# Value products of 32x64 tiles issued in six parts per pair, with a new order of issue and a new bank table

## The chip, the cores and the metric

The kernel runs on one core of one Trainium2 chip. The metric is the device time of one execution in microseconds; three runs of the kernel before gave 941.70, 940.48 and 942.59, a median of 941.7. The profile comes from a further execution, of 943.45 us.

## The reference, cut to what matters

Eight batches of eight heads, 576 rows, head size 64, all in float32. Attention keeps only the scores within `tau` of the row's maximum; a gated MLP with a spatial mix follows on the heads put side by side.

```python
scores = q @ k.T / 8
thresh = scores.max(-1) - tau
p = exp(where(scores >= thresh, scores, -1e9) - scores.max(-1))
x = p / (p.sum(-1) + 1e-9) @ v                 # (8, 8, 576, 64), then heads side by side: (8, 576, 512)
h = gelu_tanh(x @ w_in)                        # 1024 wide: u, v = halves
v_n = (v - mean(v)) / sqrt(var(v) + 1e-6) * g_ln
out = x + (u * (w_sg @ v_n + b_sg)) @ w_out
```

## The kernel before, in words

Two heads make a pair, so there are 32 pairs (`n` = 0 to 31), four for each batch. The function `attention(n, g0)` makes the steps of a pair, `moe(b, m0)` those of a batch's MLP. A step is a small closure with a kind: `at(kind, time, fn)` appends it to a list named `plan`. Nothing is issued at that point. At the end `issue(plan)` walks through `ORDER`, a packed table of step numbers written into the file, and calls the closures in that order; each engine's queue gets its instructions in this order and works them off in it. `FIRST_BANKS` is a second packed table that names, for each tile of PSUM in the order of its first use, which of the eight banks it lies in (`bank` one bank, `two_banks` two neighbours). So the order on every engine, the DMA queue of SyncE (SP) among them, is written out by hand ahead of time, and semaphores keep it safe where a tile or a bank is used again.

The pairs 4 to 30, 27 of them, work by rows (`by_rows`). A pair has nine tiles of scores (`scores`, L543: matmuls of 128x128 weights with 288 columns, four or eight for a tile, into two banks). For each tile VectorE (DVE) takes the maximum (L552), GpSimd (POOL) the threshold (L558), ScalarE (ACT) the exponential (L579), DVE the selection with the row's sum (L586), and DVE transposes 32x32 blocks into the tile `turned` (L596), of which there is one buffer. When all nine are there, `turned_values` (L743 to L751) multiplies with `v`: 18 blocks of 32 keys (`NB`), four row groups of 32 partitions (`NG`) and two heads, 144 products with weights of 32x64 and 144 columns, each of which the trace shows as two matmuls and two weight loads. Eight such tiles fill the array side by side. Their sums go to four banks, `accs`, as two tiles of two banks. After the last, DVE scales the sums by the inverse row sums (`scale_turned`, L757), and ACT and POOL split the result into a high and a low part for the MLP. The loads of the next pair's `v` go into the same buffer as this pair's.

The MLP's products (`products`, L843) are issued in steps of up to four matmuls of 128x128 weights with 288 or 512 columns, of kinds v, u, y and o; the order puts them among the steps of attention, so that TensorE (PE) works on the MLP of one batch while the pairs of the next are in the softmax. In the order before, the whole of `turned_values` is one step, and its 288 matmuls follow each other in PE's queue.

Of the kernel before, what the change touches and what calls it, by code (L numbers as in the profile page):

```python
# [32 lines left out]
ORDER = (  # L33
    "c-mE12S8L;7X9ZB^Zo$C0D>Y_!LDG#j%>_oG#V^vx{8_@Q`MN=O-$dIvMH`5MNKqoOpGOoCYp#QF|J0VV#P+W0HPE{Q2H?Q|KPlR<<CF{_~pG@&OP_O`"
    "`(}^3Z+zD_zx5>yRwgbm3LD_ksmoDN5mYvdi@h^MX3}Jzh1OHD~kWwf2Tfa3g0+{IY<~n&8xsG<iK4*g65XxBWNqu){B=rmx9ci*R;omz3fd`;x4_?q="
    "X{nsWixhz1*yn5TP<7Vw7tu)Ms5dU}H=IR5%l4LWsyeel_vPz=cshB;6?j6wGk_iI5@+pAmu*sE=VUq#3U16;`NX`k-bee1IW6Dn7RFz|4plvv45&K|="
    "E(P<${!16^D>P*GgerYKH<T=51ugPcNx+Ss_urcjr^NSGW|niYj<DmLn}xfEM7e>Tww372$Z6L^HW%_ZOqV@!ix`JBtNrAXms8^^&M2z_SRtS@PYicxQ"
    "n%f!HExO=I~KkS(+QI1Jq73iF*FG1X>B2}o6aJ81BO>wHysxye0r2?f)3pGKAfT_RYT{fw2vU*1qR!wv~U}?Z6fbrMXi1?!vpo*=vI9&b(X%iZPUJ;D+"
    "$0exL6?vh)^~W7a$PBJaCW+@vIP|T4Ati|w<~bMswqP^K5bW_ko2zx<3$7Gb+eV;hE*~{*djxlA5-Tyeq!SU0%#nzgN_&Dqtu>R>gr~TCtWZ<kChJHz6"
    "r%Farnp5;IUqkk*}Axd=90!-z6R(^zsZI`EWNp;hM5YP7*W-xd09G&xfV<VRQc1d-?U=pT%nrVEM6*@kr=7J^V+DtZ@Q?z4ivL0SZsnFUn(>=AJyE{AE"  # L40
    "!CaS>QiR*v+Q7nwx5zPPdrUs9T2Rmd&0`xuqFKl#M;|5vI%LxTw4_QB9b2o6h+wo7A|LTanQGo=t1a6qOhy7JqGM;>qn>hYXc8>Gt#CGpD&ZJgXtY(4<"
    "GV=IemmvYY2tar>F%D&kEzWY4B^@hBqo$E^quKC6lhl6$2Bo-`t+-O|7CD6I%<G7ExqO~xa0shQZ!tJ^F_O~lW%1iu0umF%0?ByHS?o61a@D?&0P(&v`"
    "wWoAT9WtsS#2t6v3MEz6<I?P>Nh)4`FZrVz_nKBs&mE~gwtthf|s3bx{lO&kPxqxJo-KpDOl2S`Z`&g5|{xUZK3edh)pvebmUu)$+Fs3QGS@|+4V%qF)"
    "LP(OL6aJt}s}h6a_CfLmpt%)a48Eo&QtUr<h<Y>GqP`j;X5d6Ivnr_4+ti9gMCJPPC6O~DCx~uFF9w((kwV-H(P?V|%VdgQv52KPvwZz)-Xxx9R<ff}-"
    "Ph`fPTXzIZCqV9Q_enw@>k;aZ4Vrnm}4l+JP2K#j}W)7%9$89%&!W+F*Aa0ZpvqcjZq=O-l^_CArfIryb2uL0N0aArGJ7US)qFCNs{Qk!vLpAlhd3(-M"
    "9DfaS;_aEMaj~b6#51iRsK2iP=TP14ko<{BM#Z{@kWFOGXsktQ;aGbRujM37fr8!I6L=p%X!rqWibwHivM|q;zD)C3zsSm<11JZa8utpDwCJ=0YY!#7J"
    "e30=(|uzD3kT#v;chZ^D?2>CY#55tT?EC9Nx@RiFA0`oYT!HzZe|coDEf+&VQm5cxKXPgV|9`~@Wo#(Yp@fhiKZF7|W@O8^urU6w`bb}C<mKS{Q*AWcy"
    "p7NP0OT$}GfK5avIAd0`VsX#?_vsC4vAe9)>2vZWd@HrOoQ=feqoh*Dmod)%7N{WvdQE~oywweotnuTB{l=_+v)qM*?=7}0I(~?i|V=iKyaA#J<paK*1"
    ")quYSiCibtmrUw&q)^3VR1j#@rKBuBvtCSmikxAFt%gL+12DK(_N2>K$_5N`>tSN-#;#Uh3e3gQdWd5&2_t5LtvVCucZ0KIaE6#cVMMr-lycYxZS#H0b"
    "U{sj{KxEi{E;hC;l#?FNmhl5Ap#MTRz;G>B)A#hZYBMiFGlP4Y@chtBN?M%l`jU@5y0E9;yVU$6at}Qz8S(fALKe#6Q_?9L8m$7Ywl)LB4oi8HGB{h>D"  # L50
    "M&p-yRGzMTTs3T+J#oYx?IV1S^JQL5TPbv?*D`w{cK&o<Cbf4RD6|jVD!RQ1D~wOAWJTT6r{NF8<sw|J17d-KnhrZF8r8lJ@U_wDmtCZT^KpX&W!5gzw"
    ")Et^Y&up{A`%z;DnGp8gq2t0CI<zX7eW98)pOOVyK;oX+DzW@ZoVu3kI%wZ#Ht>}esMV8G=Vx-Vo{lk+m^6nqF)fTSNER#YEWKWJ}K6?B`mWzjpY{?Zu"
    "i$W6Kw+O6qkeQI6gh$HGLBmu$YcBlPXV!I-1OJaqB`@f3_Lv~E?lw}=AP)T4&bzsNlgrZL81^}m@zSMlHqIUx#g3hb)<O<xd#VQS<4MwEZYK4ci97RIs"
    "^;6QGUvW6mnOHD(Z8r+_YCmW3T}_37YE)chi8rEKz{R3L(HHyIME=j)wF*Hk<hBj&xSF6l?ts8Mp2)NDg->mbvy<BiKrNxSZ`bwFiw7I8FRitc;NQoTS"
    "<2LC%Yb6<jnv<JdxK*0Y63!&H_is?8}~m_-*~4qHMoBJW6k+Pntm7sVE?28si*I$?SQJnyIWY_+cA;scw=|kab?edPz<`b{lNhrjm4IC4<a=hH*!M5y*"
    "oySdo9hk`hUK#_;$a*3ViknP;g>Ihw2Nx4?S=_wz|XiN2@_fuVv(SB)UfnP#t;Dg3y9ys0Zh+M<gbGnPJ17m>b5f$iI<V;E9ago5{_vZ)dlB^GNNJ6RS"
    "?V6O~_;Tkyr>-vidq=9NbgPXnxuNZ{#3%v9YU7!!MI{oFg&c1<HIF83%&dd&UF4MIF56xFe-o;CjY;nIHt&T<DncyrmS@4tU1;FU+!@Z>)tSd>9=b2i+"
    "M4%OIJZf|#y<-Z#cWt0G~JG<81-lfi7vT)@~UlsOvB>!|lpQh42<*08reh(dwUst|^hO*EG+yO#^D&ra(;wlE?V!b-FJOtj+HMth3r-wFO7}^w2AKnW)"
    "9cX|f?t-JSSH(L&ms?^cthvzlDmvp_bftsk0zEGGal_RYD$~o=Kugi7i&2&vnqJy9kCczWW%OV(hw4LYI?Mio6QqR%e!gte?2T7Z+YX3mng21nbtH!&K"
    "BJ*t>J7J%Z%fSs3kzv^N$Tk#%9&|o?7UtJS9Z(ldJ-egB?lnB#Ci%&jB0eC<ISpYqRyU%gp?zWMrI|_<(j;+CN>#+9_6_78;8`9nd-sM9S`LV+^Kt^2E"  # L60
    "%DbQ^?}C5pPKBIs>-7M~uC2*tV(1dN=K}>67<NJv!q*<Jjc32p~<}F|}}l^@9ghw`vm_YaiXPIBVs|$M@a!VKhRTm<-PL7#5}8j`T*>MqfEF_wKQ;x;`"
    "zL_v_z&c^vZx0u7;GK30$CSc28JU;bkK%!S5V?;BrZBr?@a`2Jzcc%&%wd9paPL0`dS+@FDX=97<}A^FqJ5>G@Evmf;Cv({ceP1(6B=KfvJWBF@wkK>J"
    "i=3sOz){NkH?%>T@9!$ycpEs7cSG=}(V+o>1K~)c)O(t`pLtE5SAg9KVEy&Ec@)a4luaXXfdUO_kgd>Daw&Z8eQ|Y5aPU3TC_?%S{ShjQD7;SHSx#giB"
    "T(fF`aNv&;>q=Ia`+?2GJ|pcpI_EmW=4i}Yuv#5;sJQEu_+e+dI&$u2gQbpSYYSfOT-tT?=Tp)D)oJ}(${Ip}y@OAwmj35}^#2Wpa*FiBQ)^UEduAFCL"
    "qhVC%cfAzuZS&M{m0Ri^JzFXe0A!X)VkmRHRl=ZAAN#|IC`E?lTc~&KRSX506B(pQ26--wKP5eY1u(}-flf{{&HVdf@#<_a5zq&E3QPKD$3DVty0y&n7"
    "N}K#4Il|rX#vCA$<#aCSGNzndv}YjAfyrIaBDnDI>vJ9t{1K!yN}y%W{cAZn!ht84}{Pczaz&vH^01@zC6bO&50?et@(mfZpvON&khJsyvL@4D-PKcGa"
    "TN+K4=E|8LZ?kA#R&%8_t#$gNPrehpai@{%Q2G5ObVMY-X19ugaogZ@Tg%Rnx7azIQOsW-w&3rhcTt+RUqi(x}!P(bl0%YHP+p<l5P*ie?7NDZ~1Y~rR"
    "h8!PJK%QYi|JHg&pa*pb@0X8E$1Z74q#4LZ1!|2--l9!T~a`w9qcx@D&>OOlXGIrJsa25hXPNrJaV`&0oAz$z4l~81lx*TlSiy57>{=UlluONG9bY-+^"
    "xzc3~x&Vv!ll`Oj<I=s^pKWUDPJSPKa!A_I%`DpT>xj8g%p6WFtV5VhN6v^a5@Kko#cB5(8v1S0Uz5kaW8WW^6m0Cmw5<c#y6%mJA0x6BCU2O1R;80F*"
    "cv#CZNNjrJKo$eRx{26Ls@ES3cgQ&`WCXU-$LZG4C=Mcue`l@DGI;OdMXWTmX8Ov=KX8Wy*po9u0Jqh(Xt;fY6XwmF{j;%=dmJT3y|r}m^WqTbhe+~E_"  # L70
    "{JaEiGOP%onMFvAF>R+Wlm!ZpVxqq#B=vvaN8@`nm2kfzK>i`Q}qlqbiN19Z=(#XFM@5Y|f2#wp9V>g+qUt3U%J<SHfStb~yc!r@ZO-BUAO{**D;A^+k"
    "=Kk+qE_g4(_($?MofzX^xBa@SeoWz3BxrG5VSp_{z$QAz=;J&)aJ30{EZD;S6CXa?JCR()#NaOf@z8p0OFJ(^sm2JG9$=x504c9c0o@VevUvW2S`Eej9"
    "KZ2plaHlrpGflIpErnC6Ieq_^-&f8{g=Ho3Sv&a?n-`N}A(i*OX>-t9CjzjEt_)CV&!=<;)z}EY})9!x}D^4RNCu1JdinhX9`^JC0mM6YoM(*2H-@O_x"
    "HSQLkV12bIWW>w3`_q?py@hR4=XAoz|Ne70?#$WvMo)wt5bd+MPk2bf$uVqmIZQ6i-k5oMz}e2%?m{2ndkuP2eOPG95d}H<F*ne)_!+j-V51$FvXl9;u"
    "njb9^J{y@?ob0VejB&jY7rDVJ)y>53%egNYD*@M`z^~m91owupqxR6ZggqiX=`0-bMQr@Tl4rUr9tg0;!5wjikrL!npq>TSTW#4)ZxSFtZT6Tg9=Mw_d"
    "8B|Ocm`2bkc46g4KTR%R}mI=Yvk9<atu8eRktssBA;aQ|JFin*q&moEie;9Zb7K6O#)xi!(Lsgp)Oxb~h5#>rt_dIA`s1!blfwQUf`r#xl$uVosG~NR?"
    "XBH}PuX_YarUbwHOtNdJ=F0bir3FNU62zU^|Y%us%ey(odzA~fXov*1js1)bgHKtN(qi=pPGI$vA$>?c-Pu3BT4yl|&AjyHVhl}P$&%9WtT3sfB%Sz&9"
    "i8%em{*z;0I=7Az~uMbmeZ-z#)5D=_3RnOc!V|N6za=TiqPtNbpJy#WlBAPX+yrF2w*5>X;jmG*nx+JoL!cDdbBa&31Lk?!b*t2qRR1@*YhE~ne)#zw!"
    "XSjkrO;Mg0+$y*SWt}YS%-WKbVQdS#A3xvsbLXDTWmoUL1YTw8##1xBMlM?vgLjV)*yjqm`=l`8NX?JoU6R#h*W&hLP9|5Y_h!tmqx~=R!I_)?upkf35"
    "jfsgh5I6gT3lz79qQ(&^!Va+Lxuz#Juwt1c2)m{Z8rVR_hO8dM+YP{*mpmg6`z2PywR&mBc>zmz}n|mELgq3V_zRv5m)h;d)4NJH7}@i8Nwg`0{GCvI!"  # L80
    "WgHuP@{^^Rb6~8D1Anh-N>Y%wr8u8_D#IL90_kS1;J#ooz5x50To#lQ|FTLz?Dp2(;C`P*xuvpw{+%^DXzSJx{!iH{UlN`F7Wl3%!lyi<V8p+7Dit`W$"
    "nyot=?T6Y<>A$@}q@$`+j5u2u5<-fv>sy$eiEV7>ai*BOm1FTLZ6gvUd^2ClFbU2=4U%EWb>S{14u938a;b5z~-(bX@1?ykKD-k6J6nm1tVv%{ZX5kBe"
    "3k%vxZwu|Eg=z$M@H7ar2)c4{a`r#p5&-T2?f~?)NaM@gJdT}XRAk*`cf!r;bTUa4X{2+NEel(t{3n%MR{<3N^I^mP6Sa@~tCg{&%z0>xjv6eh-TiW7S"
    ";0Au3{GZ?_v=3QLJcjkglfPxr&uqJ}?w-!;?jkR-lUu{?(wEl-m%>GQqOgYx=LU>AGAKJOXBzOG`ysF|Jl~AW?iYvJcx;)pE0;BjgbKAAnqYS_GVpKpV"
    "{`xHZLpD$iAyGX$WN2TEl41>Q4`tMoo}Z{vmMFdp40g9jH%a8^>CajWYV3PZmuOEeOn8OR|n%H8!AdvM|?eI|7f7Zn9NQ9t~C$rc%UKWU3og}o;&zlG^"
    "_h|*1e=7!uSz0;3hU7S-Wv2-6HxWhUGFU@Ga&#OPcrzf+SwN!Hz&XKiz{P!Gxr0#@>k3)7)4U85N>46V}FK@i#k;-!S~3EjChbs_3T=K43viw#x_`e2X"
    ";3UAMbq?ChHt+@2)?!;jE4=a7=!qtSYB7G2*nx{{q!yu2mkGyk1NvcvMBTOFuc7INRu81CGX!luro#PEJl`Hy)PIub<_D}S0)UlYihO@V7riF?HHMu*y"
# [20 lines left out]
WARM = 4  # L110
# [1046 lines left out]
```

## Time and profile before

| | |
|---|---|
| median of three runs | 941.7 us |
| profiled execution | 943.45 us, its span 941.5 us |
| PE busy | 849.7 us (90%) |
| DVE busy | 701.0 us (74%) |
| ACT busy | 605.4 us (64%) |
| POOL busy | 587.1 us (62%) |
| mean granted PE clock | 0.978 |
| value products, PE | 7,776 matmuls, 146.9 us busy, 56.4 us idle ahead of them |

The span runs from the first to the last instruction. Busy time is the union of an engine's instructions; matmuls overlap each other, and their ends are modelled, so a matmul listed with 0.28 us can be followed by the next after 0.016 us. "Idle before, releaser" is the time in which an engine did nothing ahead of an instruction and what ended it; "issue" means that nothing the profile shows ended it.

### The profile page before, as it was taken

The page shows a single profiled execution, that of the slowest core. Times are in us where ns is not written, and L with a number is a line of the kernel's source. Part 1 is how long each engine was busy: PE and PEld are TensorE (multiplying, and loading weights), DVE is VectorE, ACT ScalarE, POOL GpSimd, SP SyncE. Part 2 cuts the span into 40 slices and gives each one's busy share as a digit, 9 for nine tenths or more (in the row PEclk, how much of TensorE's full clock was granted, in tenths as well). Part 3 has the DMA queues.
Part 4 walks back from the last instruction along what each step waited for, and adds up shares of the span by engine and source line. Part 5 has one row for each costly group of instructions (what it writes and reads, how often), then busy time and mean ns, then how long its engine had stood idle before and what let it go on. Part 6 is the DMA issues. An engine that isn't in the chain of part 4 may idle for free.

```text
span 941.5 us, 30436 instructions
## 1 busy us (share of the span) xinstructions
PE 849.7 (90%) x12440; PEld 761.2 (81%) x12440; DVE 701.0 (74%) x1436; ACT 605.4 (64%) x989; POOL 587.1 (62%) x973
## 2 busy tenths in 40 slices
...
GB/s 248 177 73 104 130 104 88 149 159 112 156 126 158 169 170 84 117 163 129 145 103 137 125 133 134 162 110 135 127 128 150 139 121 153 99 84 28 32 7 52
DMA packets 71998, 115.79 MB, mean 123 GB/s; under 512 B 10033, under 2 KB 32049, under 8 KB 71858
## 3 DMA queue, kind: packets, MB, share of 16 engines
...
q8 instruction: 98, 1.61, 0.7%
...
## 4 chain that ended last, share of the span: by engine, by line
PE 66%; DVE 10%; issue 10%; POOL 6%; ACT 6%; DMA 1%; SPq 0%; POOLq 0%; DVEq 0%; ACTq 0%
PE all_banks L843 34%; PE all_banks L750 15%; PE all_banks L543 11%; DVE nm L552 3%; DVE p L586 2%; DVE turned L596 2%; PE all_banks L239 2%; PE all_banks L738 2%; ACT p L579 2%; POOL klz L445 1%; PE all_banks L521 1%; POOL ot L1050 1%; ACT L832 1%; DVE ir L757 1%; ACT L579 1%
## 5 line engine op out<-in xcount | busy, mean ns | idle before, releaser
L579 ACT ACTIVATE p<-all_banks,nm 128x576 f32<-128x576 f32 x256 | 184.1, 741 | 91.0 <-DVE nm L552 89.5
L586 DVE SCALAR_TENSOR_TENSOR p<-all_banks,nm,p 128x576 f32<-128x576 f32 x256 | 201.9, 806 | 49.7 <-ACT p L579 29.7
L552 DVE TENSOR_REDUCE nm<-all_banks 128x1 f32<-128x576 f32 x288 | 207.6, 743 | 18.8 <-PE all_banks L543 11.8
L750 PE MATMUL all_banks<-turned,v 32*64 32x144 f32 x7776 | 146.9, 290 | 56.4 <-issue 54.2
L750 PEld LDWEIGHTS all_banks<-turned,v 32*64 32x64 f32 x7776 | 128.4, 133 | 71.9 <-issue 66.9
L596 DVE STREAM_TRANSPOSE turned<-p 128x576 f32<-128x576 f32 x216 | 159.9, 759 | 31.8 <-PE all_banks L750 31.7
L543 PE MATMUL all_banks<-ks,qst 128*128 128x288 f32 x560 | 164.0, 312 | 13.5 <-DVE p L586 9.1
L558 POOL TENSOR_TENSOR nm<-columns,nm 128x1 f32<-128x1 f32 x288 | 53.3, 192 | 188.4 <-DVE nm L552 155.6
L543 PE MATMUL all_banks<-klz,qst 128*128 128x288 f32 x560 | 157.5, 300 | 0.3
L543 PEld LDWEIGHTS all_banks<-ks,qst 128*128 128x128 f32 x560 | 107.8, 192 | 25.5 <-DVE p L586 12.7
L843 PE MATMUL all_banks<-wsh,z 128*128 128x288 f32 (+2 forms) x512 | 112.8, 301 | 1.5 <-DVE p L586 0.7
L543 PEld LDWEIGHTS all_banks<-klz,qst 128*128 128x128 f32 x560 | 108.1, 193 | 2.1 <-POOL klz L445 0.9
L843 PEld LDWEIGHTS all_banks<-wsh,z 128*128 128x128 f32 x512 | 86.6, 193 | 2.8 <-DVE p L586 1.0
L445 POOL TENSOR_TENSOR klz<-rk,khi 64x576 fp32r<-64x576 f32 (+1 forms) x56 | 80.0, 1429 | 8.4 <-PE all_banks L543 2.5
L832 ACT ACT_TABLE_LOAD x52 | 66.7, 1283 | 26.8 <-PE all_banks L843 17.6
L843 PE MATMUL all_banks<-gh,woh 128*128 128x288 f32 (+2 forms) x256 | 76.6, 302 | 0.7 <-DVE p L586 0.4
L843 PE MATMUL all_banks<-gh,wol 128*128 128x288 f32 (+2 forms) x256 | 76.4, 301 | 0.0
L843 PE MATMUL all_banks<-xh,wih 128*128 128x288 f32 (+2 forms) x256 | 75.7, 301 | 0.6 <-ACT vv L832 0.6
L843 PE MATMUL all_banks<-wsl,z 128*128 128x288 f32 (+2 forms) x256 | 75.8, 300 | 0.0
L843 PE MATMUL all_banks<-xh,wil 128*128 128x288 f32 (+2 forms) x256 | 74.9, 297 | 0.0
L843 PE MATMUL all_banks<-xl,wih 128*128 128x288 f32 (+2 forms) x256 | 74.6, 296 | 0.0
L843 PE MATMUL all_banks<-gl,woh 128*128 128x288 f32 (+1 forms) x240 | 71.6, 301 | 0.0
...
## 6 DMA issues: line engine op xcount, KB each, us to landing
...
ks<-khi SPq DMA_DIRECT2D x110, 144.0 KB
...
```

The costliest lines, as they stand in the source:

```text
L239: nc.tensor.transpose(out, x, ident_r.bitcast(F32))
L445: nc.gpsimd.tensor_tensor(klz[h][rows, 0:w], st["k"][rows, o:o + w], st["kh"][rows, o:o + w], ALU.subtract)
L543: nc.tensor.matmul(sc[:, a, 0:HALF], w, x, start=(j == 0), stop=(j == len(terms) - 1))
L552: nc.vector.tensor_reduce(nmax, st["s", h, i][:, :, 0:HALF], AX.XY, ALU.max, negate=True)
L558: nc.gpsimd.tensor_tensor(thr, toff, st["nm", h, i], ALU.subtract)
L579: nc.scalar.activation(target(h, i), st["s", h, i][:, :, 0:HALF], AF.Exp, bias=st["nm", h, i])
L586: nc.vector.scalar_tensor_tensor(dst, st["s", h, i][:, :, 0:HALF], st["thr", h, i], dst, ALU.is_ge, ALU.mult, accum_out=st["l"][:, c:c + 1])
L596: nc.vector.transpose(st["turned"][:, :, o:o + Q], st["p", i][:, c0:c0 + S].rearrange("p (k x) -> p k x", x=Q))
L738: nc.tensor.matmul(acc[h * D:(h + 1) * D, 0:w], st["v"][:, o:o + D], unit(h, a)[:, kt, 0:w] if kt < NM else tail_unit(a)[:, 0:w], start=(k ...
L750: nc.tensor.matmul(accs[g // 2][hs, g % 2, 0:W], st["v"][rows, o:o + D], st["turned"][rows, k, h * W:(h + 1) * W], start=(k == 0), stop=(k ...
L832: put("gelu", end, lambda: nc.scalar.activation(tile_of(), acc_of(), AF.Gelu_apprx_tanh))
L843: nc.tensor.matmul(st["acc"], *term(j), start=(j == 0), stop=(j == n - 1))
```

## The change

`turned_values` takes a range of the 18 blocks of keys, and six steps of three blocks (24 products each) take the place of the one step. The accumulators are taken at the first part and stay until the scaling. The plan grows from 4,543 to 4,678 steps, and both tables are new.

```diff
+PART = 3
...
-        def turned_values():
-            accs = [two_banks(f"pv{n}_{a}") for a in range(2)]
-            for k in range(NB):
-                for g in range(NG):
-                    for h in range(2):
-                        rows, hs = slice(g * Q, (g + 1) * Q), slice(h * D, (h + 1) * D)
-                        o = k * P + h * D
-                        nc.tensor.matmul(accs[g // 2][hs, g % 2, 0:W], st["v"][rows, o:o + D],
-                                         st["turned"][rows, k, h * W:(h + 1) * W], start=(k == 0), stop=(k == NB - 1))
-            st["accs"] = accs
+        def turned_values(k0, k1):
+            def f():
+                if k0 == 0:
+                    st["accs"] = [two_banks(f"pv{n}_{a}") for a in range(2)]
+                for k in range(k0, k1):
+                    for g in range(NG):
+                        for h in range(2):
...
+                            nc.tensor.matmul(st["accs"][g // 2][hs, g % 2, 0:W], st["v"][rows, o:o + D],
+                                             st["turned"][rows, k, h * W:(h + 1) * W], start=(k == 0), stop=(k == NB - 1))
+            return f
...
             if by_rows:
-                at("pv", g, turned_values)
+                for k in range(0, NB, PART):
+                    at("pv", g, turned_values(k, k + PART))
```

What the new order table says of these steps, decoded: in 100 of the 135 seams between two parts of a pair nothing else is on PE's queue. In 35 there are other matmuls: 4 of them in three seams, 8 in seven, 12 in sixteen, 16 in four, 20 in two, and 10, 14 and 18 in one each, 406 in all. Twenty pairs have one such seam, six have two and one has three. In 33 of the seams there are scores of the next pair among them, in the others only products of the MLP. For pair 15, for instance, PE's queue reads: scores (0,0) and (1,0) of pair 16, parts 0 to 2, scores (0,1) and (1,1) of pair 16 (eight matmuls), parts 3 to 5, scores (0,2) of pair 16. The scores (0,1) lie in the banks of the scores (0,0), the scores (1,1) in those of (1,0). In the order before, all four stand ahead of the value products. On each engine the other steps stand on average two to four places from where they stood.

## Rows read from the trace of the kernel before

**Rows 1.** The page's first part: busy us (share of the span) xinstructions.

```profile
PE 849.7 (90%) x12440; PEld 761.2 (81%) x12440; DVE 701.0 (74%) x1436; ACT 605.4 (64%) x989; POOL 587.1 (62%) x973
```

**Rows 2.** The chain that ended last, shares of the span by engine.

```profile
PE 66%; DVE 10%; issue 10%; POOL 6%; ACT 6%; DMA 1%; SPq 0%; POOLq 0%; DVEq 0%; ACTq 0%
```

**Rows 3.** Waits: engine, line, waited for: us in total, times, longest us.

```profile
PE all_banks L750 <- issue: 54.2, 36, 3.0
DVE ir L757 <- PE all_banks L750: 45.6, 17, 4.9
...
DVE turned L596 <- PE all_banks L750: 31.7, 11, 5.5
...
PE all_banks L543 <- DVE p L586: 9.1, 8, 3.0
```

**Rows 4.** Timeline of PE, 643.6 to 655.2: start us, us, what [idle before].

```profile
644.13 2.72 PE L750 MATMUL all_banks<-turned,v 32*64 32x144 f32 x157
648.58 2.25 PE L750 MATMUL all_banks<-turned,v 32*64 32x144 f32 x128 [1.73 <-issue]
653.15 0.46 PE L750 MATMUL all_banks<-turned,v 32*64 32x144 f32 x3 [2.31 <-issue]
```

**Rows 5.** Timeline of PE, 371 to 375.5.

```profile
371.59 2.25 PE L750 MATMUL all_banks<-turned,v 32*64 32x144 f32 x128 [1.12 <-issue]
375.04 0.50 PE L750 MATMUL all_banks<-turned,v 32*64 32x144 f32 x15 [1.20 <-issue]
```

**Rows 6.** DMA queue, kind: transfers, MB, share of 16 engines.

```profile
q8 instruction: 98, 1.61, 0.7%
```

**Rows 7.** Timeline of PE, 184.2 to 192.2.

```profile
184.57 0.29 PE L543 MATMUL all_banks<-ks,qst 128*128 128x288 f32 x1
184.70 0.29 PE L543 MATMUL all_banks<-klz,qst 128*128 128x288 f32 x1
184.93 2.97 PE L750 MATMUL all_banks<-turned,v 32*64 32x144 f32 x173
188.98 2.17 PE L750 MATMUL all_banks<-turned,v 32*64 32x144 f32 x115 [1.09 <-issue]
191.08 0.40 PE L543 MATMUL all_banks<-ks,qst 128*128 128x288 f32 x1
191.32 0.29 PE L543 MATMUL all_banks<-klz,qst 128*128 128x288 f32 x1
```

**Rows 8.** Line L750: duration ns min/median/max, first and last start us, form.

```profile
L750 PE MATMUL all_banks<-turned,v x7776: 277/281/497, 128.6 to 859.3; 32*64 32x144 f32 x200
```

**Rows 9.** By stretch: length; busy (xcount) of PE, PEld, DVE, ACT, POOL; granted clock; DMA.

```profile
163.30:166.70 3.40, 3.40 (x73) 3.02 (x58) 1.23 (x2) 0.00 (x0) 0.00 (x0) 0.51 0.14 14
...
654.90:658.30 3.40, 3.40 (x16) 3.40 (x15) 2.56 (x6) 1.97 (x5) 1.90 (x4) 0.50 0.46 162
658.30:661.70 3.40, 3.40 (x28) 3.40 (x27) 2.85 (x6) 1.93 (x5) 2.28 (x4) 1.00 0.46 116
...
794.80:798.20 3.40, 3.40 (x16) 3.40 (x16) 3.25 (x6) 0.68 (x3) 0.77 (x2) 0.50 0.62 162
```

**Rows 10.** Groups: xcount | busy us, mean ns of one | idle before, releaser.

```profile
L579 ACT ACTIVATE p<-all_banks,nm 128x576 f32<-128x576 f32 x256 | 184.1, 741 | 91.0 <-DVE nm L552 89.5
L586 DVE SCALAR_TENSOR_TENSOR p<-all_banks,nm,p 128x576 f32<-128x576 f32 x256 | 201.9, 806 | 49.7 <-ACT p L579 29.7
L552 DVE TENSOR_REDUCE nm<-all_banks 128x1 f32<-128x576 f32 x288 | 207.6, 743 | 18.8 <-PE all_banks L543 11.8
```

**Rows 11.** By stretch: all 27 value blocks, and a stretch dense on DVE.

```profile
128.60:859.60 731.00, 656.74 (x11180) 610.37 (x11180) 568.11 (x1142) 461.52 (x698) 448.53 (x729) 0.97 0.47 131
300.00:400.00 100.00, 93.58 (x1589) 87.56 (x1588) 84.69 (x171) 72.07 (x109) 69.72 (x113) 1.00 0.51 141
```

More of the change, by code (lines that the diff above doesn't have):

```diff
@@ L33 @@
 ORDER = (
[L34 to L87, printed above, removed]
@@ L88 @@
-    "=jLi9^99DK3szCbT^wSM@XAMGO@XXDz*Lq_5dx417VQu<rR+lRK&@G5VIUYVrn#$0N<)FBu9r?3<Y&VkiY<4)+>Y}uBv6@!LRt973%s@|&TPaN{Vc+ja"
-    "Lj<0hH-+w|NmTWO8Afn?aSMWt7S^F`EO&kLlh@son5)HA?z_jsl!3TwXz60b-~)Ce4WIWR{D|4e*4(iXH)3wYUdUwiyLR(z@9yZz7zd7pT?V@KqQ^!Y1"
-    "^bf9b|+FW6qg*a7yH0%A@#uyutQjSPDG=lPeG5%39K_8pYoHMk<~YAer447wdL{Uh`SgP9L~<&H4%I6jp0eR7IrU;`DA-G8*`G=!*W;@NY2-7m)WMZ9B"
-    ";DfohVL`E5YhGbn&<uz>Lx)3-m?vKXs&KC(%x<G((!VKe&EY7BJEIJI0;>#$iu7U9|fHe*EJ*gx+cC%ob<(&EKM`x`XdYc2*i>+SX}mz!xA|^@P}U>f_"
-    "}n^$|(u$?xdE)Ow)@(bX&aF!~Tf6xjXBod6dh_o>?%M-wJLLlZg{z&=4eKj0S_O>E&RC6ltOxHro^7426qz*jL!W%R72U>*C*n2sQ7*f~0|B`?06ss_N"
@@ L93 @@
-    "xc#LcBX8hObJsWmB7|NO(0(Gi>I%jw0CLp6d@P4pX`^*oxyJPhq$oTB<S9;%cC6+cJ2CmSnTNmR!*t9txM{0&v+*N#~n-sWpQs7UHYPM$B;h7ECAT~1A"
-    "=^osR$O?7<Wv6QEVOGaa0za^_j^zTSKs>**19_(g_7#!IIlBes_GLFVdWp4$Sm!}Zz=hry#^4wn6&S<%+mSIhuAP}v2lLaZ0ZEQ(hrzbO;$B6p3trILJ"
-    "9PW`I8AFT?_!j92`cJ_0`xBNFyT0x&a13R8>bmy^a2+(X{CT&dIA@^mg~K63+_O7AY42ML%RhevL_ZRGyi{avoF&"
+    "c-mE133wCL7M?R{?o65{Z7HQKZCSctX$uGxq#*bN!6%zg5J8`Spnxdiz96`M`rMw%Q)J%+!39*1@(=_!6j@3UC`)%*3bX}E(lp6T(%g6My)$V|!(`^(v"
+    ";5~j=bn29Num;dDF0zs3KFG~`NuBpu74X3-$00&knl>y5M{q046}PS7uE`YsrUj7@qv&zVPY}VxnaCPFA(B$AutfK5iSD)9-lC$@e1L%3{hb`1i}&iGT"
@@ new lines @@
+    "$Iva6uZ9jmUss1$?H3!XawNQV?TcXmgv)1ow%q*ex3|P=kmi1ZLFy4h0NDA?}Ua4YlzjBB2J2T+1*<IR+jo`xgQu8g>zXl9^N^yZphB45!mDz$_aeMWB"
+    "Kh&R)1O@M4oBk0b;+n~V^<m*TM3<^gukP}#gT2?yEL=54Dg{8Ld7A8`u*jPy$E4*$>qDhM}h%428ac<cRp*)e%EYm<EFmm5bp=8(;BV>WJ<-FSr(vuiV"
+    "mK)W70_1gFy$8G1J1PU%|V;ChK6psNPywt2jHbcFf4nEN;GbJyM;l-yi$J`zN^6)s-UTzw(N;V%g3tJK&)1R0B3zxpl2tkBx6FLH^p~>)akE+*ZvSc$8"
+    "=2NMU6De$>h|k7(5jjzjKQ74K(6)3)B1@>@Q@w%)b3q!5m#Tgy!}vEQZ9Z-YBcm9ejVXrLIU~i#t@_L*ErrWlTvT6p+#p5>Q)7x%0k^^9WfSO+&9LYxp"
+    "TRo}m_;qI0UCBgO@q`&)pqVtNj1V@irhN0jdxs(jdD9Glk|llsw{oNITgbykItw1Om~7DHiBa+L*x?xDKqU8Vd0b##>wY|EB;HlPeGDu@FzHtc+kwE>J"
@@ new lines @@
+    "#CZM$~Yp^NF?1af!?^93nL4mkQJEdH{2%a!Us1)bMF0gn=;K8*VsR)C9+5I2tptYM2e-Rghss;uFlZD>+L23gsjyeoEVygR%A%@g$g({HmWN)fa}tlj#"
+    "$2OB}zT+s73-*NVY0k42Cqs@<nZq6FG9$(I%T_|3XE;}rSl!Lk?>zv5?>@QPvz7xfzj!mzL!VnS@f&&9+O=Z-%jNUqC%@mVo==LQ*gKR3%2{Jeuwzi1u"
+    "d8fRKK!iG66W|S%-mqyWZlxU4fay#solc4&AEoQ{e)es)K;GPwZ*=MFf@f&1wLw?$BXAmPidF<Y#LqOr-Q$8w!r((ivfy@m~P&VgRgffC)eDLfmf;>?j"
+    "f*7-Om^;RwB6#u(W)weFOoYOtKiqBwT56tCc!rsG7Nx?=kY(M7htb4SCK;3o=Zg51xNkE(JSGmtOp4#M!f+ZWggTXs#0u7!IWwom0^&k`?p~CGVmgp`h"
+    "9r|3$%sC@QiO9}_guy-Kk-bBYzgy5it(OkOoN(9HIgApkO}a-aCw#(Gs}u(CWbRD7OJ^s+HD&Wvu|=>e!_VXG#KT_tCLW%NJQQ_7h;uANiwU5)1$R*g~"
@@ new lines @@
+    "Z=hpA4tQbI%G`(#+a13PdP~ylG-pn*6sv<%)5%Y(h~qVn7zrVo*4#30oS`SVBd`;HVKS>iETSCY(Qwn<il<xIS$wF2cjpm}wIL<%3*~n5{tZ6S1xd!=x"
+    "Fd&5hv*`@>s;s+x!k!4Z5Q61ObzUn(NgB&jV|2ABLt<5?p#EX37#12VS`{1VE>m^gEa84>=&Cr2XaZ{O4@AEsPR#3u=yhMF0uCSakEh=fm5!y;#h+u@d"
+    "2*lbpq6dW6O91b<gkZ5M#B4(Ltw9OnB5g>W^f=I!aFew-j+(;&JL)%!qglkiie<Q`zh>zK#ta1dyZT#{?5*~q3R#fEH;EtG14I;Q3!jr)5Qf`FuB#Ue?"
+    "dnU7H=uCjS*NBl-Gar)RHM}c}QjsJPH!(1xj8&)9xaYA-Ces|JRnl3TAx1;vj4@MID*O@385c$=uNc9nz}N0*EWA+7EIk7dmlv8wwNtJATd62VUY1&0N"
+    "uipKS1Z5OtsEFb#WO@Doke9XxA2PM(NGlDg&<F~m8HmBio7mF*RZ0H7FMP#T~s%+s<k^m6Vau^z01mMh6~6lYzhtZZq==neF?*%3*L1$h4)sGaz=(2;u"
@@ new lines @@
+    "ot<+g|w?PTiyv1<b<XqiB%|RpC}Q_eB;8^DG>47#Iq3z(80TgOtH)lM(E(8_F>=NhZkrP_D^E*)P*(bhW*hN~SyRglCQl-o@GwKG_X5V&PsSo=I+u=xj"
+    "vz)D4Uhm(h7_lJKav{YOW5k1{|oo~(NKP1CBkdxKym7)qXr@PA_HX0zg?a0;kkQW9}<mu(x4^!H<})b1rE+<na>IW;eBdnj$M@V7T8+O~21&3IV7U7(b"
+    "jhoAQEpl!<LsjQvxzu&cq{0*5U1b@g7il7#NyiP4seg^rL%|||b@y^20KL+gJw+-_YM|d1TH*{zQRa1u?9#rni0(-fO^eI#2%Y%03kzjNMSTd{9j(LV0"
+    ")0LY}4Q^_QYKcBYzzLowziTP5{1B9zQ|lU{2Ub-;y0b!#=}_Zn(eB$8Ogr8&wT^Z<KD>zpsS7$@bCN)f><1zzyQ8gE@VaXH$^McqT}Z<>Pj^NjxffbVl"
+    "ag2Fxsci8j5m_B*5<h~PbVDfeKDhncsjWvgWYP?dR<K+FWfazm814~h#VOJ@WiFm1)~-Hw{b2~9iO?Udjiy7j!tVjkuFE&{?@5%9DFw8tn-?7&YBU`^F"
@@ new lines @@
+    "lXRe@9v04o#k*x4wtFctU_Qcu&ZS*U0hyG;+1ektBeWZ&FSd{0wkMQzsw+@|`DZGHgqh8hVobX(^;*lw;@JJK=caOGVKC&52+Ir|kN1jIE-3^R;nTu5T"
+    "NYVynB*{Ro`_P}=EgY4Bf%NbtynKYC=ibO>6lQji29<QL{P6n=C%rOpcWRt>+u%w7kx))&a&>$VlH73eY64G)6ti|MOp-iRfEEz{-CcMhDjbMlFg@0|k"
+    "Z@vfbS>nd2&pc0hG8-wbXjQ{?PItAno_4YtnPWMt>v3@x<8e*<CEl*hR@)8m`ch!y9mN%cP|Li4a>s$5DgIA8tJ=nb>E_U|EA&}PqTm<`)7dHSDz&G<?"
+    "J>1ih`EltR0E^$G8`%A1d&3WpEqe?;anD~qA3l9?>_30#Esx(Zo)#={cs@P@&PO1LyfFXm7e76G6l4p?H{uF5mkjhp>JOI`O@OaR)0K%Zycrx&*5eaRb"
+    "uV(kW=ogaOejgOeQa5elHMTauL;awn>HLGewwUmpn&$eyYFyV-P#N8Tb!GJ#BUp^0{CE`Mh2{&w{i|GcqRjOz%xzI2<+3?<G0BThkJAY`1y7KT{$!uU@"
@@ new lines @@
+    "5@+-y9lzD2dd(6uoic7b+qf1F&z@u6tqKR8;y#mm{BlPd|1m!#q6jfu&$Oozx2_ww>>l0##$boUZS={pay1XXApfVutd4w_(3QUJ-`((ZW8#sFq;N$0V"
+    "m>LPV7BE0_}VOGz(gCUA!1xyjn=r0fJa1#09BSUXc*50F@&>VN?dI&K;LKRJ7c?8+gT0BHafhwWtaevcj}xa&P;m!{}SYwNB_U-uzFB5P`j0#JEVDJ07"
+    "DN@sfjivUh!*v@ndX{se2;JR`u&nr{;mVN55HS<<JyawI0cpRPt?`g!+C8}AD>i?&r6g?OsJI9@<BMuwDc?)gI4Mm_sO>RkomWr5!Y{X8yXxmCHEjXpf"
+    "`vzHYq~+wWh5uE$SBKK8(*7dZm5KH;Ij0EJ3?Ro9=rLjii@2K{k^g7Dj6DYi9K!|yyT|;>#uJGHz?nXA$42luZ1N;})B=AF##PXgimNO+iN)+b4L3VHK"
+    "aH9H;f|+jQ>sIezSanWy8gZ6=Pum`BNvWycpSsvVm^)`;3F^IKNRNB88g;``zd{s8%Lu6i>nzh>&=zve>u|q=cj+`aZF@<zJL@*O(b7=5Qlr!v+jS9Qv"
```

42 lines of the change are left out of this document (38 added, 4 removed).

## The prediction

> **What bounds the kernel now.** I read the busy line, the chain, the list of waits, then the timeline of TensorE (PE) inside one block of value products, and last the clock by stretch. PE is busy 849.7 of 941.5 us, the next engine, DVE, 701.0 [rows 1]. The chain is 66% PE, and 10% of it is "issue", time in which the engine waited for nothing that the profile shows [rows 2]. So PE sets the time, and its idle time is the thing to look for. The list of waits has one large entry for PE: 54.2 us in 36 waits of L750 on "issue"; the next, scores waiting for DVE, is 9.1 us in 8 [rows 3]. L750 is the line of the value products.
>
> The timeline shows where that is [rows 4]. A pair's 288 matmuls (144 products, each two records) start at 644.13 and run 157 long; PE then idles 1.73 us, does exactly 128, idles 2.31 us, and does 3. Between the idle times lie 128 matmuls with their 128 weight loads: 256 instructions. Another pair shows the same 128 [rows 5]. The instruction queue has 98 transfers of together 1.61 MB, 16 KB each; PE has 24,880 matmuls and weight loads [rows 1, 6], or 254 per transfer. I read the idle times as PE running out of fetched instructions: it consumes a block of 256 in 2.0 us (128 matmuls, 15.6 ns apart: 172 steps in 2.97 - 0.28 us, the length of the last one [rows 7, 8]) and gets a new one only 3.45 us (371.59 to 375.04 [rows 5]) to 4.57 us (648.58 to 653.15 [rows 4]) after the last one began; I use 3.9. In the 128x288 matmuls, 0.13 us apart, a block lasts 17 us, and nothing is missing. The Trainium skill, "Runtime: NRT & Kernel Launch", section "Instruction fetch mechanics", has the same block (16 KiB, 256 instructions), but calls the crossing "mostly hidden"; by that these idle times would have another cause and stay, which is the last rival below. The trace agrees on the block and not on the hiding.
>
> Some stretches right behind such idle times run at half the clock: from 654.90 us PE does 16 matmuls at 0.50, in the next stretch of the same length 28 at 1.00 [rows 9]. I found eight such stretches behind blocks of value products (the first and the last stand in the rows too).
>
> **The change part by part.** The sum is made against the profiled execution (span 941.5 us, 943.45 us in all, 1.75 above the median of 941.7); I carry the difference over to the median.
>
> *The split itself* adds no instruction: six parts of 24 products are the same 144. What counts is where other work enters. Decoded, the new order interrupts the 27 blocks 35 times, with 406 matmuls in all, 12 in the commonest case (16 times), 8 in seven, 4 in three, 10 to 20 in nine; the other 100 seams between parts have nothing in them.
>
> *Stalls removed.* The 36 idle times are counted from the modelled end of the last matmul, 0.28 us after its start [rows 8], while the next should have started 0.016 us after it: 54.2 + 36 x 0.265 = 64 us. With m wide matmuls inside a block, PE takes (128 - m) x 0.0156 + m x 0.132 + 0.40 (the price of the interruption, below): 3.8 us for m = 12, 3.3 for 8, 2.9 for 4. Against 3.9 that leaves 0.1, 0.6 and 1.0 us in place of 1.9. Over the 35 interruptions this is about 9 us. But the block boundary must lie so that the interruption falls between two of them. Counting two instructions per matmul through the new order, with wait instructions as dense as before, nearly every block that lies inside value products holds one; one has none, and several hold only the smaller of two: 14 us remain. If the boundaries fell anywhere, it would be 28. I take 14, from the count: -50 us, bounds -36 and -55.
>
> *The clock.* A half-clock stretch loses 12 matmuls of 0.13 us [rows 9], 1.6 us; eight are 13 us. They follow idle times that mostly go; I take -10, bounds -4 and -13.
>
> *Interruptions added.* On the way in, the first value product starts 0.23 us after the last wide matmul (184.70 to 184.93) in place of 0.13. On the way out the next wide one starts 0.21 us after the last value product (191.15 - 0.28 to 191.08) in place of 0.016, and the one behind it 0.24 us later in place of 0.13 [rows 7, 8]. Together 0.10 + 0.19 + 0.11 = 0.40 us, and 35 of them +14 us, all of it on PE. It is what speaks most against the change: with other work in all 135 seams it would be 54 us and eat the gain. The Trainium skill, "TensorEngine Tiling (Array Packing)", section "Key Properties", says that a change of tiling mode drains the array; the 0.40 us agree, and the page has no price.
>
> *New waits.* In 33 of the 35 interruptions the work put in has scores of the next pair in it, often written into banks that the two scores tiles just ahead of the block still hold, since the accumulators keep four of eight banks until the last part. Such scores wait for max, exponential and selection of the older tile, 0.74 + 0.74 + 0.81 us [rows 10]; queued behind them on PE are the remaining parts, and for these wait DVE's scaling (45.6 us now) and the first transposition of the next pair (31.7 us, [rows 3]), as `turned` has one buffer. What covers it are the two or three parts ahead, 1.5 to 2.3 us: just enough if DVE starts when the older scores end. Today a wait of scores for DVE costs 9.1 / 8 = 1.1 us [rows 3]. Also a faster PE leaves DVE less slack: it is busy 568 of 731 us from the first block to the last [rows 11], 78%, and would be at 82%. From 0 to 20 us; I take +8, about one wait in four interruptions.
>
> *Order and banks elsewhere* are shuffled by two to four places in each queue, SP's loads too. The loads of `v` for a pair still come behind the last value product of the pair before, which comes no later, and the waits list no PE time lost to them. I put this at 0, bounds -6 and +6.
>
> Sum: -50 - 10 + 14 + 8 = -38 us: 905.5 us for a profiled execution, 904 us at the median.
>
> **The rivals.**
> *All of it pays* (nothing new is waited for, the half-clock stretches go, 10 us of stalls remain): -54 - 13 + 14 = -53, 889 us. For it: DVE's two waits on value products, 77 us, shrink as well. Against: some interruptions are too short.
> *The boundaries fall elsewhere*: wait instructions in the new order shift the blocks, 28 us of stalls remain and half of the clock's loss: -36 - 6 + 14 + 8 = -20, 922 us. For it: the count depends on some hundred and fifty wait instructions whose places I can only assume.
> *DVE takes over*: if it can't be denser than 80%, 568 us need 710 in place of 731: -21, 921 us. Against: from 300 to 400 us it does 84.69 in 100 [rows 11].
> *The banks hold PE (slower).* If DVE reaches the older scores only when the interruption begins, each of the 35 waits the whole 2.3 us: -46 + 80, 976 us. It decides from 46 / 35 = 1.3 us per interruption on. For it: the cover is thin, and today's longest such wait is 3.0 us [rows 3]. Against: those scores come 2 us and more ahead.
> *The idle time is not the fetch and stays*: only +14 + 8, 964 us. Against: the 128 matmuls between two idle times.
>
> **How the numbers follow.** Forecast 0.50 (its own range 895 to 914), all pays 0.17, boundaries 0.15, DVE 0.08, banks 0.06, not the fetch 0.04. The range 884 to 930 us takes in the first four with their spread and leaves out some 0.13. About 0.2% is what a measurement here can tell from no change. The two slower cases give 0.10, the lower ends of the middle ones 0.03 for no change, 0.87 for faster.
>
> **What would show it.** Right: PE's wait of L750 on "issue" falls from 54 to some 5 to 12 us; DVE's waits for L750 fall; the clock has one to three half-clock stretches behind value products; each interruption still shows about 0.2 us in and 0.2 out. Wrong: idle times still 128 matmuls apart with no other work between (boundaries), or PE's waits of scores on DVE over 30 us (banks, DVE). The forecast fails if the time is above 930 us, or if it is met while "issue" at L750 is still above 30 us.

## The result, and the profile after

The changed kernel takes 908.42 us (median of 4 runs, 908.23 to 908.68), the kernel before 941.09 (the three runs that were known and a fourth of 934.05); the ratio is 0.9667, 95% interval 0.9619 to 0.9716. The forecast was 904, the range 884 to 930. The profiled execution took 908.68 us, its span 906.9.

The page's first part, after:

```profile
PE 852.6 (94%) x12440; PEld 752.9 (83%) x12440; DVE 702.9 (78%) x1436; ACT 601.4 (66%) x985; POOL 588.3 (65%) x973
```

The chain that ended last, by engine:

```profile
PE 45%; DVE 18%; POOL 12%; ACT 10%; issue 8%; DMA 5%; SPq 2%; POOLq 0%; DVEq 0%; ACTq 0%
```

The work is the same, PE's busy time too [rows 1]; the span around it is 34.6 us shorter. The chain has less PE and more of the others [rows 2]. The waits of PE, as total us, count and the longest one (L750 before is L755 now, L543 is L546, L757 is L762):

```profile
PE all_banks L546 <- DVE p L589: 7.4, 17, 1.1
PE all_banks L849 <- issue: 4.4, 3, 2.6
...
PE all_banks L755 <- issue: 2.5, 2, 2.3
...
PE all_banks L546 <- issue: 1.2, 1, 1.2
```

Those of DVE on the value products:

```profile
DVE turned L599 <- PE all_banks L755: 3.2, 3, 1.7
DVE ir L762 <- PE all_banks L755: 2.5, 6, 0.8
```

PE's 54.2 us on "issue" inside the value products [rows 3] are 2.5, and 5.6 more now fall on wide matmuls behind them (L849, L546), at the end of a block or inside an interruption. DVE's 77 us of waiting for them are 5.7. The timeline of PE in pair 15, an interruption of eight matmuls in the middle:

```profile
409.71 0.29 PE L546 MATMUL all_banks<-klz,qst 128*128 128x288 f32 x1
409.93 2.54 PE L755 MATMUL all_banks<-turned,v 32*64 32x144 f32 x144
412.50 0.40 PE L546 MATMUL all_banks<-ks,qst 128*128 128x288 f32 x1
412.74 0.29 PE L546 MATMUL all_banks<-klz,qst 128*128 128x288 f32 x1
...
413.53 0.40 PE L546 MATMUL all_banks<-ks,qst 128*128 128x288 f32 x1 [0.24 <-DVE p L589]
...
414.03 0.29 PE L546 MATMUL all_banks<-klz,qst 128*128 128x288 f32 x1
414.25 2.51 PE L755 MATMUL all_banks<-turned,v 32*64 32x144 f32 x144
416.88 0.40 PE L546 MATMUL all_banks<-ks,qst 128*128 128x288 f32 x1
417.11 0.29 PE L546 MATMUL all_banks<-klz,qst 128*128 128x288 f32 x1
```

No idle time within the 288 value matmuls, and 0.24 us on DVE between the two halves; the way in takes 0.22 us again and the second wide matmul comes 0.24 us after the first, as before [rows 7]. Two idle times of over 2 us on "issue" are left. One lies in pair 8, behind the first matmul of an interruption:

```profile
231.79 2.51 PE L755 MATMUL all_banks<-turned,v 32*64 32x144 f32 x144
234.23 0.40 PE L849 MATMUL all_banks<-xl,wih 128*128 128x288 f32 x1
237.26 0.29 PE L849 MATMUL all_banks<-xh,wil 128*128 128x288 f32 x1 [2.63 <-issue]
```

There the block of 256 holds 127 value matmuls and a single wide one. The other lies in pair 19:

```profile
518.14 2.51 PE L755 MATMUL all_banks<-turned,v 32*64 32x144 f32 x144
...
521.84 2.52 PE L755 MATMUL all_banks<-turned,v 32*64 32x144 f32 x137
526.68 0.47 PE L755 MATMUL all_banks<-turned,v 32*64 32x144 f32 x7 [2.31 <-issue]
```

The 128 matmuls that end at this idle time all lie behind the interruption, so this block has none. By stretch, all value blocks and the three stretches at half clock among them:

```profile
128.00:824.80 696.80, 659.47 (x11187) 602.88 (x11186) 572.30 (x1142) 458.96 (x695) 453.46 (x734) 0.99 0.50 138
249.30:259.50 10.20, 7.63 (x29) 6.94 (x30) 9.99 (x22) 7.91 (x11) 7.95 (x14) 0.50 0.14 43
471.10:474.50 3.40, 3.40 (x16) 3.40 (x16) 3.30 (x7) 1.54 (x3) 1.75 (x3) 0.51 0.09 21
529.20:532.60 3.40, 2.90 (x12) 2.90 (x13) 3.40 (x8) 1.41 (x2) 0.38 (x2) 0.50 0.30 102
```

The whole gain lies here: 731 us [rows 11] became 697; ahead and behind less than 1 us changed. I sorted the distances from each matmul's start to the next in this stretch: the usual distance of its kind (0.016 us for value products, 0.13 for 288 columns, the ways in and out as they stand), and what is over it by cause. Each row is good to some 3 us, the changes to about 1.

| us, first to last value product | before | after | change | forecast |
|---|---|---|---|---|
| usual distances, interruptions among them | 613.0 | 628.3 | +15.3 | +14 |
| idle for instructions, in or just behind value products | 65.5 | 11.2 | -54.3 | -50 |
| lost at half clock | 15.3 | 6.1 | -9.2 | -10 |
| other waits of PE | 37.1 | 51.4 | +14.3 | +8 |
| sum | 730.9 | 697.0 | -33.9 | -38 |

### The profile page after: what moved, and what is told of

It is laid out like the page before. It is cut to its first block, busy times and chain, and to the rows that moved or that the text cites. A ratio compares the mean times of both kernels' runs of the same rounds, so it can differ in the third digit from the quotient of the medians.

```text
span 906.9 us, 30418 instructions
## 1 busy us (share of the span) xinstructions
PE 852.6 (94%) x12440; PEld 752.9 (83%) x12440; DVE 702.9 (78%) x1436; ACT 601.4 (66%) x985; POOL 588.3 (65%) x973
## 4 chain that ended last, share of the span: by engine, by line
PE 45%; DVE 18%; POOL 12%; ACT 10%; issue 8%; DMA 5%; SPq 2%; POOLq 0%; DVEq 0%; ACTq 0%
PE all_banks L849 26%; PE all_banks L546 8%; DVE nm L555 6%; DVE p L589 5%; PE all_banks L755 4%; DVE turned L599 4%; ACT p L582 3%; PE all_banks L242 2%; POOL ot L1056 2%; PE all_banks L741 2%; POOL vv L950 2%; PE all_banks L524 1%; POOL klz L448 1%; ACT L838 1%; POOL z L963 1%
## 5 line engine op out<-in xcount | busy, mean ns | idle before, releaser
L589 DVE SCALAR_TENSOR_TENSOR p<-all_banks,nm,p 128x576 f32<-128x576 f32 x256 | 202.4, 808 | 51.7 <-ACT p L582 30.8
L555 DVE TENSOR_REDUCE nm<-all_banks 128x1 f32<-128x576 f32 x288 | 207.7, 742 | 34.6 <-PE all_banks L546 23.9
L546 PE MATMUL all_banks<-ks,qst 128*128 128x288 f32 x560 | 166.1, 316 | 19.1 <-DVE p L589 7.4
L546 PE MATMUL all_banks<-klz,qst 128*128 128x288 f32 x560 | 156.8, 298 | 1.6 <-POOL klz L448 1.5
L755 PE MATMUL all_banks<-turned,v 32*64 32x144 f32 x7776 | 142.3, 286 | 3.8 <-issue 2.5
L755 PEld LDWEIGHTS all_banks<-turned,v 32*64 32x64 f32 x7776 | 123.1, 130 | 17.6 <-issue 13.8
L546 PEld LDWEIGHTS all_banks<-ks,qst 128*128 128x128 f32 x560 | 106.4, 190 | 36.6 <-DVE p L589 16.8
L849 PE MATMUL all_banks<-wsh,z 128*128 128x288 f32 (+2 forms) x512 | 114.1, 302 | 3.2 <-DVE pm L589 2.6
L546 PEld LDWEIGHTS all_banks<-klz,qst 128*128 128x128 f32 x560 | 106.8, 191 | 4.9 <-POOL klz L448 3.0
L849 PEld LDWEIGHTS all_banks<-wsh,z 128*128 128x128 f32 x512 | 86.5, 192 | 5.5 <-DVE pm L589 3.2
L849 PE MATMUL all_banks<-gh,woh 128*128 128x288 f32 (+2 forms) x256 | 76.9, 303 | 2.7 <-DVE ir L762 1.3
L849 PE MATMUL all_banks<-xh,wih 128*128 128x288 f32 (+2 forms) x256 | 75.2, 298 | 2.1 <-DVE p L589 2.1
L849 PE MATMUL all_banks<-xh,wil 128*128 128x288 f32 (+2 forms) x256 | 74.1, 296 | 2.6 <-issue 2.6
L849 PE MATMUL all_banks<-wsl,z 128*128 128x288 f32 (+2 forms) x256 | 75.8, 300 | 0.0
L849 PE MATMUL all_banks<-gh,wol 128*128 128x288 f32 (+2 forms) x256 | 75.3, 297 | 0.0
L849 PE MATMUL all_banks<-xl,wih 128*128 128x288 f32 (+2 forms) x256 | 74.6, 296 | 0.0
L849 PE MATMUL all_banks<-gl,woh 128*128 128x288 f32 (+1 forms) x240 | 71.4, 299 | 1.8 <-issue 1.8
```

Of the source, the lines that this page charges most:

```text
L546: nc.tensor.matmul(sc[:, a, 0:HALF], w, x, start=(j == 0), stop=(j == len(terms) - 1))
L555: nc.vector.tensor_reduce(nmax, st["s", h, i][:, :, 0:HALF], AX.XY, ALU.max, negate=True)
L589: nc.vector.scalar_tensor_tensor(dst, st["s", h, i][:, :, 0:HALF], st["thr", h, i], dst, ALU.is_ge, ALU.mult, accum_out=st["l"][:, c:c + 1])
L755: nc.tensor.matmul(st["accs"][g // 2][hs, g % 2, 0:W], st["v"][rows, o:o + D], st["turned"][rows, k, h * W:(h + 1) * W], start=(k == 0), s ...
L849: nc.tensor.matmul(st["acc"], *term(j), start=(j == 0), stop=(j == n - 1))
```

## The experiments

All times are medians, and ratios are to the kernel before on the same chip; it takes 937.7 to 940.0 us on the chips used here. The changed kernel's 908.42 us comes from another chip; on that of runs 5 to 7 it takes 907.65 (run 5). "Issue" is PE's wait on it at the value products.

**1. Blocks made whole again** (parts 1 to 5 moved up to part 0):

```diff
+        for first, *rest in parts_of(plan):
+            for i in rest:
+                order.remove(i)
+            at = order.index(first) + 1
+            order[at:at] = rest
```

> The order and banks of after, but parts 1 to 5 of each pair moved up right behind part 0, so that what stood between them comes behind the block. Fetch theory (PE runs out of instructions after 256 of them inside a block of value products): some 35 idle times at L755 with 128 matmuls between come back, by the block count 62 us in place of 11, the 35 interruptions (13 us) go, some half-clock stretches come back: 940 to 955 us. Rival (the gain comes from the new order and banks elsewhere, the interruptions do nothing): 905 to 912 us.

Measured: 1033.02 us (1032.28 to 1041.67), ratio 1.1058 (1.0975 to 1.1141). Neither theory had this. The waits, PE's on issue and DVE's largest:

```profile
PE all_banks L755 <- issue: 51.9, 35, 2.8
...
DVE nm L555 <- PE all_banks L546: 139.0, 55, 8.7
```

One stretch at half clock, with the columns of [rows 9]:

```profile
528.00:541.70 13.70, 9.90 (x55) 8.82 (x44) 8.61 (x17) 8.63 (x12) 5.77 (x11) 0.50 0.13 31
```

The 35 idle times are back as the fetch theory had it. But the scores that stood in the block are what DVE works on during it, and now DVE waits 139 us for scores where it waited 23.9 in the changed kernel. PE then waits for DVE (18.9 us at the scores and 18.5 at the MLP for the selection, L589, where it was 7.4 and 2.4), and runs at half clock for 109 us between the first and the last value product in place of 17. By the same sorting as above PE loses about 55 us more to instructions than in the changed kernel, 34 to the clock and 45 to other waits. So in this order the interruptions do two things, and the run doesn't measure the first alone.

**2. More interruptions:** the first part of the next run moved into the middle of what stands between, 27 times.

```diff
+                if len(between) >= 2 and empty:
+                    order.remove(ps[j + 1])
+                    order.insert(order.index(between[len(between) // 2]), ps[j + 1])
```

> After, with 27 of the 35 groups of other matmuls cut in two by the next part, so 27 interruptions more with the same other work. If an interruption costs PE 0.38 to 0.40 us: +10 us, and by the block count +3 us of stalls: 919 to 923 us. Rival (the price of an interruption is hidden, PE catches up): under 911 us.

Measured: 919.55 us (918.51 to 922.05), +11.1 on the changed kernel; issue 6.9 us in 7. From the first to the last value product it takes 710.2 us in place of 696.8; the usual distances grow by 10.2 of this, 0.38 us for each of the 27, the idle time for instructions by some 2. PE does not get it back.

**3 and 4. The same order with other boundaries:** 80 PE instructions more in the warm-up, and as a control 256, a whole block.

```diff
-            nc.tensor.matmul(x[:, 0:2 * P], pm[:, 0:P], pm[:, 0:2 * P], start=True, stop=True)
+            nc.tensor.matmul(x[:, 0:P], pm[:, 0:P], pm[:, 0:P], start=True, stop=True)
+            for j in range(PAD // 4 if k == WARM - 1 else 0):
+                hs = slice(j % 2 * D, (j % 2 + 1) * D)
+                nc.tensor.matmul(x[hs, P:P + 16], pm[0:Q, 0:D], pm[0:Q, 0:16], start=True, stop=True)
```

> After, with 80 more PE instructions in the warm-up (20 products of 32x64 by 16 columns; the four warm-up products have 128 columns in place of 256), so that all boundaries of 256 instructions shift by 80; nothing else moves. Fetch theory: the interruptions no longer lie where the blocks need them, the count gives 32 us of stalls in place of 11, and a few half-clock stretches: 928 to 937 us. Rival (what counts is only that each block is interrupted in its middle): 907 to 911 us.

> The control of the one before: 256 more PE instructions in the warm-up, a whole block, so that the boundaries lie as in after. Fetch theory: 908 to 912 us (the longer warm-up may delay the start by up to 3 us). If padding itself costs time: as much as with 80 or more.

Measured: 924.48 us (920.36 to 926.99) with 80, 914.44 (912.32 to 918.12) with 256, ratios 0.9864 and 0.9765. The waits, first with 80, then with 256:

```profile
PE all_banks L759 <- issue: 22.5, 18, 2.4
```

```profile
PE all_banks L759 <- issue: 7.9, 6, 2.7
```

The steps behind the warm-up are the same in the same order; with the boundaries shifted there are 18 idle times at the value products, with the control 6, in the changed kernel 2. The time with 80 is 3.5 us below what I expected. The control is 2.4 us above: its first value product comes 4 us later than in the changed kernel, and its idle times are somewhat more.

**5 and 6. The changed kernel again, and without its four warm-up products,** 16 instructions less:

> The changed kernel itself, on this chip, for comparison with the next two: 908 us.

> After, without the four warm-up products (16 PE instructions), so that all boundaries of 256 instructions shift by 16 the other way; the start may lose or gain up to 2 us. Fetch theory: by the block count 6 us of stalls in place of 10.5, so 902 to 906 us, and the idle time of 2.6 us in the block of pair 19 goes. Rival (small shifts do nothing): 907 to 909 us.

Measured: 907.65 us (902.50 to 912.61) and 902.77 us (898.64 to 904.15), ratios to before 0.9683 and 0.9628. Issue without the 16 instructions:

```profile
PE all_banks L755 <- issue: 1.8, 2, 0.9
```

The idle time of pair 19 has left the block, but not the run: it lies ahead of the second matmul behind the block, and is 1.40 us:

```profile
516.84 2.63 PE L755 MATMUL all_banks<-turned,v 32*64 32x144 f32 x144
519.70 0.40 PE L546 MATMUL all_banks<-ks,qst 128*128 128x288 f32 x1 [0.23 <-DVE p L589]
521.50 0.29 PE L546 MATMUL all_banks<-klz,qst 128*128 128x288 f32 x1 [1.40 <-issue]
```

All idle times on "issue" together are 3.6 us, 9.5 in run 5, and the median is 4.9 us lower where 4.5 were counted. The two ranges overlap, so I call the gain likely, not settled. This version is the fastest that I ran. PE has nothing to do until 5.10 us anyway, when the first scores' operands are there.

**7. Whole blocks with the scores ahead of them** (the parts moved back to the last run, the banks kept by the tiles' names, through new tables):

> After, with parts moved back to stand right ahead of the last run of each pair, so that the blocks are whole and what stood in them comes ahead of them (the banks go with the tiles' names). e1 left DVE without scores during the block; here it has them. Fetch theory: 54 us of stalls and some 9 us of half-clock stretches back, 14 us of interruptions gone, and up to 40 us of PE waiting for the banks of the older scores: 945 to 990 us. Rival (what counts is that DVE is fed, and scores ahead feed it as well): 905 to 925 us.

Measured: 1019.14 us (1016.20 to 1022.16), beyond both. PE's waits:

```profile
PE all_banks L544 <- DVE p L587: 54.7, 30, 4.2
PE all_banks L753 <- issue: 23.2, 23, 1.7
```

Scores ahead have to wait for the banks of the older ones, 1.8 us each time. I had allowed 40 us for that; what I left out is what follows: PE comes idle into the block, and the clock is at half for 106 us between the first and the last value product. Only 23 of the 54 us on "issue" return. In part this is because 1,514 of the 7,776 value matmuls now run at half clock, 29 ns apart in place of 16, and use up instructions more slowly; that is a fifth of them and can't be all of it, the rest stays open. Fed from ahead or not at all, a whole block in this order costs over 100 us; that part of the question, fetch alone against feeding alone, these two runs don't separate.

**8. Each interruption one part later,** with the same work in it:

```diff
+            for j in reversed(filled):
+                order.remove(ps[j + 1])
+                order.insert(order.index(ps[j]) + 1, ps[j + 1])
```

> After, with every interruption one part (48 matmuls, 96 instructions) later in its block where there is room; same work in it, same order on the other engines, one interruption fewer. The scores in it have 0.75 us more for their banks. Fetch theory: where it lies against the boundaries decides, and the count gives 31 us of stalls in place of 10.5: 920 to 930 us. Rival (any interruption near the middle does it, and the time lost is waiting for banks): 903 to 909 us.

Measured: 928.95 us (927.67 to 930.33). The waits:

```profile
PE all_banks L755 <- issue: 22.3, 17, 3.2
...
PE all_banks L546 <- DVE p L589: 4.8, 8, 1.0
```

The scores inside the interruptions wait less for their banks, 0.4 us in one wait in place of 4.2 in eleven (those outside wait longer: over the whole run, with the waits on the pair's last selection, `pm`, it is 9.3 us in place of 8.6). Yet the time is 20.5 us longer than the changed kernel's: where the interruption lies against the boundaries decides.

**9. The kernel before with the 80 instructions:**

> The kernel before with the same 80 instructions more as e3. Its blocks are whole, so each meets one or two boundaries wherever these lie. Fetch theory: the count stays at 60 to 64 us of stalls, and the time at 938 to 946 us. Rival (80 instructions in the warm-up cost the 10 us by which e3 was behind its control): 948 to 955 us.

Measured: 934.23 us (931.34 to 938.80), ratio 0.9937 (0.9906 to 0.9968).

```profile
PE all_banks L754 <- issue: 44.3, 31, 2.6
```

Five idle times fewer than in [rows 3], and 6 us less than the kernel before on this chip: the padding costs nothing. Time and idle time are both below what I expected; counted as in the prediction, with what the modelled ends hide, it is some 53 us in place of the 60 to 64. So the count was not exact for whole blocks. At this other place of the boundaries they keep most of their idle times.

## Why the prediction was right

**The idle time is the fetch, and the split removes it.** Shown. The traces have more than the distance of 128 matmuls. Number the records of PE's queue in their order (matmuls, weight loads and the waits): the eleven profiled executions, from the kernel before to run 9, have 204 idle times of PE on "issue", and 201 of them come 192 or 193 records past a multiple of 256, also where the warm-up is 16 instructions shorter or 80 or 256 longer. All but one of the 204 end 1.1 to 1.9 us after the end of a 16 KB transfer on the instruction queue [rows 6]. In the kernel before all 36 do both. Runs 3, 4, 6 and 8 move boundaries or interruptions against each other, change nothing else of weight, and get idle times on "issue" of 22.5, 7.9, 1.8 and 22.3 us, in the order of the counted stalls (32, 11, 6 and 31). The count's step that I trusted least, where the wait instructions lie, held: PE's queue has 157 in place of 149. Of the 54 us on "issue" 8.1 are left, part of it behind the blocks. The Trainium skill ("Runtime: NRT & Kernel Launch", "Instruction fetch mechanics") has the block size right for this kernel, while "mostly hidden" doesn't hold where 256 instructions take PE 2 us.

**The clock.** As forecast in size, 9.2 us. Stretches at half the clock (0.50 granted, the lower of its two levels) lie at idle times of PE of 0.8 to 4 us in nearly every case, over all runs. Before, eight of the nine stretches among the value blocks lie at an idle time on "issue", 31 of 37.5 us; after, one of three does (529.20, behind pair 19's), 3.4 of 17 us. The other two follow waits for DVE of 2.4 and 1.6 us, so the part that the fetch caused went almost wholly, and a little came for another reason.

**The price of an interruption.** Right: 0.38 us in run 2 against 0.40, and nothing hides it; in the changed kernel itself 15.3 us for 35 are 0.44 each. That 135 interruptions would cost 51 to 59 us and eat most of the gain is an estimate from these prices; no run tried it.

**New waits.** The one step mis-sized: +14 us, not +8. Scores in the interruptions wait for DVE as expected, but shortly: 4.2 us in eleven waits. The waits listed for PE on other engines and on DMA, between the first and the last value product, are 27.7 us in 41 (up to 2.4 us each), 19.4 in 27 before. Inside the blocks of value products lie 7.3 us in sixteen; the others are spread: scores behind a block whose banks wait for DVE's scaling, MLP products behind a late evacuation. Some 6 of the 14 us are in no listed wait, partly because a listed wait begins only at the modelled end of the matmul before. DVE is busy 572 of 697 us, 82%, as worked out, and doesn't bound the time. That a denser PE has less slack everywhere is what these waits look like; no run takes it apart.

**The sum.** It came within 5 us because the steps are about right, but not as closely as that looks: the stalls went by 4 us more than forecast, the waits grew by 6 more, and this cancels in part.

**What I missed.** The interruptions also feed DVE. I listed DVE's 77 us of waiting for value products as a thing that would shrink, but did not see that the new order puts scores of the next pair into the block that stood ahead of it (in pair 15 two of four tiles): without the interruptions the order is worse than the one before by 80 to 95 us (runs 7 and 1). The slower rival, banks holding PE, had its mechanism in the trace at a tenth of its price: DVE reaches the older scores nearly in time. The rival with boundaries elsewhere did not happen, but runs 3 and 8 show what it would have cost, 10 to 20 us.
